# Attention and two feed-forward layers on one core: high parts of weights on GpSimd, and other costs in the planner

## The chip, the core and the metric

The kernel runs on one core of a Trainium2 chip. A core has five engines, each with a queue of its own that it works off in order: TensorE (PE, matrix products), VectorE (DVE), ScalarE (ACT), GpSimd (POOL) and SyncE (SP, which here only issues transfers). Transfers run on 16 DMA engines; they are issued by SyncE, ScalarE or GpSimd. Those that add to what lies at their destination ("accumulating" below) are issued by GpSimd. Matrix products are summed up in PSUM, in 8 banks of 512 columns.

The metric is the time of the device for one execution, in microseconds (us). Three runs of the kernel before took 522.79, 523.54 and 525.84 us; the median is 523.54.

## The reference

Attention over 2 batches, 12 heads, 448 positions and head size 64, with scores that are capped by a tanh, and then two feed-forward layers on 896 rows (2 x 448) of width 768 with 2048 hidden units, all in fp32:

```python
scores = cap * np.tanh((q @ k.T) / sqrt(64) / cap)
attn   = softmax(scores)                  # over keys
x      = (attn @ v)                       # 896 x 768
h = x @ w_in;   g = h * np.cos(h);              x = g @ w_out
h = x @ w_in2;  g = h * (1 / (1 + np.exp(-h))); y = g @ w_out2
```

## The kernel before, in words

The weights come as 64-bit numbers and are turned into fp32 on the chip. A fp32 product is made of three faster products: each operand is split into a high part, which TensorE's faster format holds, and a low part, which is what is left; high times high, high times low and low times high are added in the bank. A split is two instructions: a copy into the faster format (the high part, by ScalarE) and a subtraction (the low part, by VectorE). `split` (line 671) records both, with `n` columns for each of 128 partitions: 768 for a block of weights, 384 for half a one, 448 or 896 for activations.

The four feed-forward products are done in stages: `gemm_in` (first layer in), `gemm_out` (first layer out), `gemm_sums` (second in) and `gemm_last` (second out). Each uses a scheme of seven products in place of eight for blocks of 2 x 2 (Strassen's, in Winograd's form), so that sums of blocks of weights and of activations are made beforehand. These sums run on VectorE or, where a list says "DMA", as accumulating transfers that GpSimd issues (`plus`, line 477; the lists `WE`, `S1E`, `S3E`, `LE`, lines 604 to 611). One of the products of `gemm_out` is taken in plain fp32 without splits (`plain_product`).

From the end of attention on, nothing is issued directly. The stages record tasks (`do`, line 444): an engine, a cost, the values read and written, a due time. TensorE's tasks come one after the other at 202.8 ns for each 448 columns, and the due times of all others are worked out back from these. `run_plan` (line 512) then plays the tasks through: whenever an engine is free, it takes the task with the earliest due time whose inputs are there and for whose outputs buffers are free. The costs in it are formulas: `act` and `dve` (lines 471 and 474) for the two engines, `dma` (line 466) for transfers, and the table `LAT` for the time until others see a result. The order that comes out is the order in which instructions are issued on the chip; there they wait for semaphores, not for the planned times. So what the planner believes of a cost sets only the order.

In `gemm_in`, three pairs of weight blocks (p = 0, 1, 2) are multiplied plainly, with three products each; the others (p = 3 to 7) in the scheme of seven. For such a pair, `blocks` (line 862) makes four sums of half blocks, one after the other (`ADDS`), and splits in between: "A" before any sum, "S31" after two of them, "S24" after all four, "A22" besides. `m1` to `m7` (from line 976) are the seven products of a pair; `m1` ends with a ScalarE copy from one bank into another, in which `m2` goes on adding. In the trace, `v` are buffers of activations or of weights, `hl` those of a high or low part, `bank` a bank, `wx` two buffers for converted weights, `wraw` weights as loaded.

Of the kernel before, what the change touches and what calls it, by code (L numbers as in the profile page):

```python
# [38 lines left out]
def tile_attention_ffn_ffn(  # L39
# [401 lines left out]
    LAT = {"X": 0, "EW": 300, "PE": 280, "ACT": 210, "SP": 3500, "POOL": 300, "DVE": 170}  # L441
# [70 lines left out]
    def run_plan(free_at):  # L512
# [29 lines left out]
        while events:  # L542
# [15 lines left out]
            for e in LAT:  # L558
                if busy[e] > now or e == "EW":
                    continue  # L560
                for t in sorted(ready[e] + (ready["EW"] if e in ("POOL", "DVE") else []), key=lambda t: (t.dl, t.n)):
# [12 lines left out]
                    if t.eng == "EW":  # L574
                        t.eng, t.cost, t.lat = e, t.costs[e], LAT[e]
# [31 lines left out]
    DUE = [220000, 236000, 252000, 268000, 284000, 300000, 316000, 332000, 348000, 364000, 380000, 396000, 1000000000, 1000000000, 1000000000, 1000000000]  # L607
# [3 lines left out]
    S1E = [["DVE", "DMA"][n] for n in (1, 1, 0, 1, 0, 1, 0, 0)]  # L611
    HALF1 = [('half', 'ring'), ('half', 'half'), ('half', 'half'), ('ring', 'ring'), ('half', 'ring'), ('half', 'ring'), ('half', 'ring'), ('ring', 'ring')]
# [11 lines left out]
    PLAIN2 = (1, 0)  # L624

    def copy(out, src, scale=1.0):
        nc.scalar.activation(out=out, in_=src, func=AF.Copy, scale=scale)  # L627
# [103 lines left out]
    def plain_product(acc, key, w, d, gname):  # L731
        NQ, QW = HK + 1, 2
        fresh = key not in acc
        if fresh:
            acc[key] = [Val("bank") for _ in range(HK)]
        banks = acc[key]
        for q in range(NQ):
            t, subs = d[gname, q]
            for k in range(HK):
                def go(q=q, k=k, v=w[q], t=t):  # L740
                    for c in range(QW):
                        cols = slice(c * DH + k * P, c * DH + (k + 1) * P)
                        nc.tensor.matmul(banks[k].buf[:, :S], half_w(v)[:, cols], t.buf[:, c, :], start=fresh and q == 0 and c == 0, stop=q == NQ - 1 and c == QW - 1, skip_group_check=True)  # L743
                pe(3.69 * QW, go, [w[q], *subs], [banks[k]])

    def product(acc, key, w, d, gname, neg=False):
        NQ, QW = HK + 1, 2
        fresh = key not in acc
        if fresh:
            acc[key] = [Val("bank") for _ in range(HK)]  # L750
        banks = acc[key]
        for q in range(NQ):
# [12 lines left out]
    def gemm_out():  # L765
# [22 lines left out]
        if PLAIN2[0]:  # L788
            plain_product(acc, "A", x11, gx, "B11")
        else:  # L790
            product(acc, "A", x11, gx, "B11")
        if PLAIN2[1]:
            for d in range(HK):
                act(S, lambda d=d: copy(kc[d].buf[:, 0, :], bk("A", d)), [acc["A"][d]], [c11[d]])
            x12 = fresh("12")
            plain_product(acc, "B", x12, gx, "B21")
        else:
            acc["B"] = [Val("bank") for d in range(HK)]
            for d in range(HK):
                act(S, lambda d=d: copy(bk("B", d), bk("A", d)), [acc["A"][d]], [acc["B"][d]])  # L800
            x12 = fresh("12")
            product(acc, "B", x12, gx, "B21", True)
        sum_g(GE[0], gx, "B11", "B11", "B12")
        for d in range(HK):
            if PLAIN2[1]:
                dve(S, lambda d=d: sub_(kc[d].buf[:, 0, :], kc[d].buf[:, 0, :], bk("B", d)), [acc["B"][d]], [c11[d]], due=clock["pe"] + 1500)
            else:
                act(S, lambda d=d: copy(kc[d].buf[:, 0, :], bk("B", d)), [acc["B"][d]], [c11[d]], due=clock["pe"] + 1500)
            T["B11", d] = split_t((lambda d=d: kc[d].buf[:, 0, :]), [c11[d]])
# [10 lines left out]
        product(acc, "C", y, gx, "B11")  # L820
# [11 lines left out]
        product(acc, "A", x11, gx, "B12")  # L832
# [5 lines left out]
        product(acc, "C", x12, gx, "B22")  # L838
# [14 lines left out]
        product(acc, "A", x22, gx, "B21")  # L853
# [434 lines left out]
```

## Time and profile before

| | us |
|---|---|
| median of 3 runs | 523.54 (522.79 to 525.84) |
| the profiled execution | 523.46 |
| its span (first to last instruction) | 521.3 |
| TensorE busy | 512.3 |
| VectorE busy | 425.8 |
| ScalarE busy | 411.5 |
| GpSimd busy | 59.2 |

The profiled execution is the one that all rows below come from. Its time is that of the device; the span leaves out what lies before the first and behind the last instruction. The ends of matmuls are modelled, so a matmul's time is longer than the distance from its start to that of the next one, and TensorE's busy time says little; gaps are to be read from starts. A wait for several things is put down to the one that came last. The clock is what TensorE was granted, as a share of 2.4 GHz. A line such as L627 is often that of a helper which many parts of the kernel call (L627 the ScalarE copy, L630 VectorE's two-operand instruction, L686 the matmul of a split product, L743 that of the plain one).

### The profile page before, as it was taken

The numbers are of one execution on the slowest core, as the hardware profiler recorded it, in microseconds if no ns is written. First come the engines' busy times: TensorE is split into PE (matmuls) and PEld (weight loads), VectorE is DVE, ScalarE is ACT, GpSimd is POOL, SyncE is SP. The second block draws the span as 40 slices with busy tenths as digits, with TensorE's granted clock in tenths as the row PEclk, the third lists the DMA queues.
The fourth block names the chain that finished last, engine by engine and source line by source line (L and its number), as shares of the span: only waits on it lengthen the run. The fifth ranks groups of instructions, "written<-read, shape, count | busy, mean of one in ns | idle before, by whom it ended". The sixth has DMA issues, their size and how long they took to land.

```text
span 521.3 us, 7217 instructions
## 1 busy us (share of the span) xinstructions
PE 512.3 (98%) x2631; PEld 420.6 (81%) x2631; DVE 425.8 (82%) x599; ACT 411.5 (79%) x581; POOL 59.2 (11%) x82
## 2 busy tenths in 40 slices
PE   8999999999899999999999999999999999999997
PEld 5444443899799998589999999999999999999996
DVE  5388997899799789999999999977879888975660
ACT  6999997699799989999877577899999755556341
POOL 0145442001101000002100011000000013200000
PEclk9999999999989999999999999999999999999999
DMA  8146464296617117599913051969989974950111
GB/s 307 57 138 189 112 208 132 86 346 170 195 19 211 58 60 266 182 341 315 220 70 122 0 152 31 354 223 329 331 312 316 348 167 75 251 132 0 54 53 53
DMA packets 26983, 91.05 MB, mean 175 GB/s; under 512 B 4473, under 2 KB 9637, under 8 KB 26949
## 3 DMA queue, kind: packets, MB, share of 16 engines
q1 hardware_dynamic: 19488, 70.89, 38.4%
q0 software_dynamic: 7104, 19.40, 16.7%
q8 instruction: 20, 0.33, 0.2%
q10 hardware_dynamic: 356, 0.32, 0.2%
q14 instruction: 15, 0.11, 0.1%
HBM read 72.75 MB, written 10.66 MB: 160 GB/s over the span
## 4 chain that ended last, share of the span: by engine, by line
PE 86%; issue 7%; ACT 3%; DMA 2%; POOL 1%; DVE 0%; POOLq 0%; ACTq 0%
PE bank L686 68%; PE po L273 4%; PE sc L239 4%; PE bank L743 3%; DMA v<-v 2%; PE sc L243 2%; PE sm L291 2%; PE po L283 2%; ACT e L251 1%; PE warm L347 1%; ACT e L257 1%; POOL v L479 0%; ACT v L627 0%; POOL sums L312 0%; ACT hl L627 0%
## 5 line engine op out<-in xcount | busy, mean ns | idle before, releaser
L686 PE MATMUL bank<-v,hl 128*128 128x448 f32 x1440 | 299.2, 367 | 0.0
L686 PEld LDWEIGHTS bank<-v,hl 128*128 128x128 f32 x1440 | 270.8, 188 | 24.6 <-issue 0.7
L630 DVE TENSOR_TENSOR v<-v,v 128x896 fp32r<-128x896 f32 (+4 forms) x110 | 107.0, 996 | 27.6 <-ACT v L627 26.9
L627 ACT ACTIVATE v<-v 128x896 fp32r<-128x896 f32 (+2 forms) x81 | 67.9, 851 | 56.4 <-PE bank L686 54.9
L630 DVE TENSOR_TENSOR hl<-v,hl 128x768 fp32r<-128x768 f32 (+1 forms) x89 | 79.5, 899 | 12.6 <-ACT hl L627 11.2
L627 ACT ACTIVATE hl<-v 128x768 fp32r<-128x768 f32 (+1 forms) x89 | 70.2, 797 | 3.9 <-DMA v<-v 2.9
L686 PE MATMUL bank<-x,hl 128*128 128x448 f32 x297 | 63.1, 371 | 1.9 <-ACT bank L627 1.9
L686 PEld LDWEIGHTS bank<-x,hl 128*128 128x128 f32 x297 | 56.5, 191 | 7.6 <-ACT bank L627 2.3
L659 ACT ACTIVATE wraw<-wraw 128x768 int32<-128x768 uint8 x61 | 55.6, 919 | 3.4 <-DMA wraw<-in_moe_w_in 2.5
L627 ACT ACTIVATE v<-bank 128x448 f32<-128x448 f32 (+2 forms) x82 | 43.5, 539 | 17.0 <-PE bank L686 16.6
L662 ACT ACTIVATE wraw<-wraw 128x768 f32<-128x768 f32 x61 | 55.6, 916 | 0.0
L479 POOL DMA_DIRECT2D v<-v x24 | 22.5, 937 | 213.2 <-DVE hl L630 108.5
L251 ACT ACTIVATE e<-sc,scap 128x896 f32<-128x896 f32 (+1 forms) x48 | 40.1, 912 | 6.7 <-PE sc L239 6.7
L665 DVE SCALAR_TENSOR_TENSOR v<-wraw 128x768 int32<-128x768 int32 x40 | 37.8, 954 | 1.1 <-ACT wraw L662 0.6
L686 PE MATMUL bank<-v,v 128*128 128x448 f32 x180 | 38.4, 365 | 0.0
L686 PEld LDWEIGHTS bank<-v,v 128*128 128x128 f32 x180 | 33.8, 188 | 2.7
L257 ACT ACTIVATE e<-e,capt 128x3136 f32<-128x3136 f32 (+2 forms) x13 | 35.2, 2710 | 0.4
L273 PE MATMUL po<-e,vf 128*64 128x448 f32 x144 | 29.4, 540 | 0.4 <-ACT e L257 0.4
L273 PEld LDWEIGHTS po<-e,vf 128*64 128x64 f32 x144 | 10.2, 137 | 17.3 <-issue 16.3
L665 DVE SCALAR_TENSOR_TENSOR wx<-wraw 128x768 int32<-128x768 int32 x21 | 20.0, 954 | 4.4 <-ACT wraw L662 3.8
L630 DVE TENSOR_TENSOR v<-v 128x384 f32<-128x384 f32 (+1 forms) x42 | 23.4, 562 | 0.3
L312 POOL DMA_DIRECT2D sums<-xs x22 | 17.5, 800 | 50.4 <-DVE sums L318 41.8
(79 smaller groups left out, 470.1 us busy)
## 6 DMA issues: line engine op xcount, KB each, us to landing
wraw<-in_moe_w_out SPq DMA_DIRECT2D x32, 768.0 KB, 5.5
wraw<-in_moe_w_in SPq DMA_DIRECT2D x29, 768.0 KB, 5.9
wd<-wx SPq DMA_DIRECT2D x16, 384.0 KB, 5.4
v<-wd SPq DMA_DIRECT2D x16, 384.0 KB, 8.4
v<-v POOLq DMA_DIRECT2D x12, 384.0 KB, 8.4
raw<-in_qkv POOLq DMA_DIRECT2D x9, 480.0 KB, 4.4
v<-wd POOLq DMA_DIRECT2D x8, 384.0 KB, 6.5
rb<-rs SPq DMA_DIRECT2D x24, 112.0 KB, 3.2
```

Of the source, the lines that this page charges most:

```text
L239: nc.tensor.matmul(ps[:, u, :S], kk[rows, cols], qq[rows, :S], start=m == 0, stop=m == 2)
L251: nc.scalar.activation(out=e32[p][:, 2 * t:2 * t + n, :], in_=sc.pop((p, t))[:, :n, :S], func=AF.Tanh, scale=scap)
L257: nc.scalar.activation(out=e, in_=e, func=AF.Exp, scale=capt)
L273: nc.tensor.matmul(po[u * D:(u + 1) * D], vf[p][:, 2 * t + u, :], e32[p][:, 2 * t + u, :], start=first and n == 0, stop=last and n == len( ...
L312: (nc.gpsimd if p < NPT - 1 else nc.scalar).dma_start(sums[p][:, y], x[y * Q:y * Q + D + 1:D])
L479: dma("POOL", kb, lambda: nc.gpsimd.dma_start(o(), b(), accum_op=ALU.add), r, w, adds=True)
L627: nc.scalar.activation(out=out, in_=src, func=AF.Copy, scale=scale)
L630: nc.vector.tensor_tensor(out=out, in0=a, in1=b, op=op)
L659: nc.scalar.activation(out=b[:, :, 0], in_=b.bitcast(U8)[:, :, 3], func=AF.Copy, scale=1.0 / 32, bias=-0.5 + 1.0 / 64)
L662: nc.scalar.activation(out=w(1).bitcast(F32), in_=w(1).bitcast(F32), func=AF.Prelu, scale=2.0 ** -112, alpha=2.0 ** 32)
L665: nc.vector.scalar_tensor_tensor(out=view(), in0=w(1), scalar=3, in1=w(0), op0=ALU.logical_shift_left, op1=ALU.bitwise_or)
L686: nc.tensor.matmul(bank, x, y, start=first and m == 0, stop=last and m == len(ops) - 1, skip_group_check=True)
```

## The change

- In `split`, the copy that makes the high part, where it has 768 or 384 columns (weights), becomes a task of a kind of its own, "COPY". ScalarE may take it as before; GpSimd may take it where the task's due time lies far enough behind: later than now, plus the difference between the cost planned for GpSimd (2.7 us for 768 columns, 1.5 for 384) and that for ScalarE, plus 1.5 us. On GpSimd it is a multiplication by 1 or -1.
- In the planner, an accumulating transfer moves 160 instead of 200 GB/s and has a lag of 1700 instead of 600 ns; VectorE's formula has the factor 1.05 instead of 1.03.
- More sums are made by accumulating transfers: the last list of `WE` (4 transfers of 384 KB), the first pair of the second layer (`S3E`) and pair 4 of the first (`S1E`; 4 of 192 KB each).
- The due times of the conversions for the last stage (`DUE`) come at steps of 12 instead of 16 us. One pair takes its last split's buffers from another pool (`HALF1`).
- `plain_product` is merged into `product`, with a list of blocks that are multiplied whole; for the list that is set, the matmuls are the same.

```diff
-    LAT = {"X": 0, "EW": 300, "PE": 280, "ACT": 210, "SP": 3500, "POOL": 300, "DVE": 170}
+    LAT = {"X": 0, "COPY": 300, "PE": 280, "SP": 3500, "POOL": 400, "ACT": 210, "DVE": 170}
+    COSTS = {768: 2700, 384: 1500}
+    SPARE = 1500
...
-        rate = 0.2 if adds else 0.38 if kb > 450 else 0.24
+        rate = 0.16 if adds else 0.38 if kb > 450 else 0.24
         cost = 350 if eng == "SP" else 900 if adds else 600
-        do(eng, cost, fn, r, w, moves=kb * 1.024 / rate, lag=1700 if eng == "POOL" and not adds else 600, **k)
+        do(eng, cost, fn, r, w, moves=kb * 1.024 / rate, lag=1700 if eng == "POOL" else 600, **k)
...
-        do("DVE", 1.03 * (95 + (0.521 if one else 1.0417) * n), fn, r, w, **k)
+        do("DVE", 1.05 * (95 + (0.521 if one else 1.0417) * n), fn, r, w, **k)
...
-                for t in sorted(ready[e] + (ready["EW"] if e in ("POOL", "DVE") else []), key=lambda t: (t.dl, t.n)):
+                free = ready["COPY"] if e == "ACT" else [t for t in ready["COPY"] if t.dl > now + t.slow - t.cost + SPARE] if e == "POOL" else []
+                for t in sorted(ready[e] + free, key=lambda t: (t.dl, t.n)):
...
-                    if t.eng == "EW":
-                        t.eng, t.cost, t.lat = e, t.costs[e], LAT[e]
+                    if t.eng == "COPY":
+                        t.eng, t.cost, t.lat = e, t.slow if e == "POOL" else t.cost, LAT[e]
...
-    GE, WE, LE = [["DVE", "DMA"][n] for n in (0, 0, 0, 0)], [["DVE", "DMA"][n] for n in (0, 1, 1, 0)], [["DVE", "DMA"][n] for n in (0, 1)]
+    GE, WE, LE = [["DVE", "DMA"][n] for n in (0, 0, 0, 0)], [["DVE", "DMA"][n] for n in (0, 1, 1, 1)], [["DVE", "DMA"][n] for n in (0, 1)]
...
-    S3E = [["DVE", "DMA"][n] for n in (0, 1, 0, 0, 0, 0, 0, 0)]
+    S3E = [["DVE", "DMA"][n] for n in (1, 1, 0, 0, 0, 0, 0, 0)]
...
-    S1E = [["DVE", "DMA"][n] for n in (1, 1, 0, 1, 0, 1, 0, 0)]
+    S1E = [["DVE", "DMA"][n] for n in (1, 1, 0, 1, 1, 1, 0, 0)]
...
     def split(n, hi, lo, vhi, vlo, src, r, neg=False):
-        act(n, lambda: copy(vhi(), src(), -1.0 if neg else 1.0), r, [hi])
+        if n in COSTS:
+            def go():
+                if t.eng == "POOL":
+                    nc.gpsimd.tensor_scalar(out=vhi(), in0=src(), scalar1=-1.0 if neg else 1.0, scalar2=None, op0=ALU.mult)
+                else:
+                    copy(vhi(), src(), -1.0 if neg else 1.0)
+            t = do("COPY", 1.03 * (14 + 0.963 * n), go, r, [hi])
+            t.slow = COSTS[n]
+        else:
+            act(n, lambda: copy(vhi(), src(), -1.0 if neg else 1.0), r, [hi])
         dve(n, lambda: (neg_sub if neg else sub_)(vlo(), src(), vhi().bitcast(F32)), [hi, *r], [lo])
```

Since the planner sets the order, the change moves instructions on every engine. In all, 67 copies stand on GpSimd (58 of 768 columns, 9 of 384), and 12 sums more are accumulating transfers.

**ScalarE, pair 3 of the first layer.** Before: `hl_89<-v_1200` is the copy for the high part of "S24", which reads what four accumulating transfers made; `bank_1047<-bank_1045` is the copy at the end of `m1`.

```order
L659 ACTIVATE wraw_1385<-wraw_1385 128x768
L627 ACTIVATE hl_89<-v_1200 128x768
L963 ACTIVATE v_1454<-v_1454 128x448
L627 ACTIVATE v_1476<-bank_1044 128x448
L964 ACTIVATE v_1454<-v_1454 128x448
L627 ACTIVATE v_1480<-xv_68 128x448
L627 ACTIVATE v_1483<-xv_69 128x448
L627 ACTIVATE bank_1047<-bank_1045 128x448
```

After, from that same bank copy on, `hl_92<-v_1205` is the copy for "S24":

```order
L630 ACTIVATE bank_1047<-bank_1045 128x448
L955 ACTIVATE v_1482<-v_1482 128x448
L630 ACTIVATE v_1504<-xv_70 128x448
L956 ACTIVATE v_1482<-v_1482 128x448
L630 ACTIVATE v_1517<-bank_1046 128x448
L630 ACTIVATE v_1520<-xv_71 128x448
L630 ACTIVATE v_1523<-xv_72 128x448
L662 ACTIVATE wraw_1367<-wraw_1367 128x768
L630 ACTIVATE v_1391<-bank_1047 128x448
L630 ACTIVATE hl_92<-v_1205 128x768
```

The copy for "S24" stood six rows ahead of the bank copy and stands nine rows behind it.

**TensorE, the same place.** Each product is six rows of the order with nine matmuls; the first of each is shown. Before: `m2` of pair 3 (bank6), then `m6` of pair 3 (bank4), the first to read "S24" (hl2_89):

```order
L686 MATMUL bank6_1047<-x3_0_80,hl0_87 128x448 x2
...
L686 MATMUL bank4_1045<-v37_1350,hl2_89 128x448 x2
...
L686 MATMUL bank5_1046<-x3_1_81,hl2_89 128x448 x2
...
L686 MATMUL bank7_1048<-x0_0_74,v50_1420 128x448 x2
...
L686 MATMUL bank0_1041<-v10_1152,hl4_91 128x448 x2
```

After, from `m2` of pair 3 on; `m6` of pair 3 reads "S24" in hl5_92:

```order
L698 MATMUL bank6_1047<-x3_0_80,hl7_94 128x448 x2
...
L698 MATMUL bank7_1048<-x0_0_74,v29_1284 128x448 x2
...
L698 MATMUL bank0_1041<-v10_1151,hl1_88 128x448 x2
...
L698 MATMUL bank4_1045<-v51_1432,hl5_92 128x448 x2
...
L698 MATMUL bank5_1046<-x3_1_81,hl5_92 128x448 x2
```

Two products of pair 4 (bank7 and bank0) have moved ahead of `m6` of pair 3.

**GpSimd, the first feed-forward stage.** Before, from the end of attention on, only issues of accumulating transfers stand there (`v_1200` is pair 3, `v_1348` pair 5, the rest belong to `gemm_out`):

```order
L479 DMA v_1200<-v_1200 128x384 x4
L479 DMA v_1348<-v_1348 128x384 x4
L479 DMA v_2086<-v_1908 128x768
L479 DMA v_2106<-v_1931 128x768
L479 DMA v_1908<-v_2140 128x768
```

After, from the same point on (`v_1205` is pair 3, `v_1259` pair 4, `v_1353` pair 5, `wx` the plain pairs; the ISA row stands there once, ahead of the first copy):

```order
L678 ISA
L678 TENSOR_SCALAR hl_93<-wx 128x768
L678 TENSOR_SCALAR hl_88<-wx 128x768
L481 DMA v_1205<-v_1205 128x384
L678 TENSOR_SCALAR v_1284<-v_1259 128x768
L481 DMA v_1259<-v_1259 128x384
L481 DMA v_1205<-v_1205 128x384
L678 TENSOR_SCALAR hl_91<-wx 128x768
L481 DMA v_1259<-v_1259 128x384
L481 DMA v_1353<-v_1353 128x384
L481 DMA v_1205<-v_1205 128x384
```

Copies and the transfers of three pairs now stand in one queue, where those of two pairs stood alone.

## Rows read from the trace of the kernel before

**Rows 1.** The page's first part: busy us, share of the span, instructions.

```profile
PE 512.3 (98%) x2631; PEld 420.6 (81%) x2631; DVE 425.8 (82%) x599; ACT 411.5 (79%) x581; POOL 59.2 (11%) x82
```

**Rows 2.** The page's slices, 40 of equal length, busy tenths and granted clock.

```profile
PE   8999999999899999999999999999999999999997
...
PEclk9999999999989999999999999999999999999999
```

**Rows 3.** TensorE's timeline: start and length in us, then [idle time before <-releaser].

```profile
93.65 45.87 PE L686 MATMUL bank<-x,hl 128*128 128x448 f32 x225
139.35 1.99 PE L686 MATMUL bank<-v,hl 128*128 128x448 f32 x9
143.24 3.35 PE L686 MATMUL bank<-x,hl 128*128 128x448 f32 x9 [1.90 <-ACT bank L627]
146.39 2.33 PE L686 MATMUL bank<-v,hl 128*128 128x448 f32 x9
148.56 1.99 PE L686 MATMUL bank<-x,hl 128*128 128x448 f32 x9
```

**Rows 4.** Windows: busy time of each engine in a stretch.

```profile
core 0: us, PE busy (x) PEld busy (x) DVE busy (x) ACT busy (x) POOL busy (x), PEclk, DMA share, GB/s
...
143.00:150.00 7.00, 6.76 (x26) 6.10 (x27) 6.35 (x13) 6.61 (x14) 0.86 (x1) 0.76 0.17 29
197.00:223.00 26.00, 26.00 (x91) 17.00 (x90) 24.81 (x34) 25.97 (x43) 0.00 (x0) 1.00 0.67 233
223.00:311.00 88.00, 88.00 (x434) 81.23 (x433) 84.12 (x102) 68.22 (x94) 8.71 (x10) 1.00 0.58 172
```

**Rows 5.** ScalarE's timeline around the gap.

```profile
139.62 0.85 ACT L627 ACTIVATE hl<-v 128x768 fp32r<-128x768 f32 x1 [2.88 <-DMA v<-v]
...
142.66 0.53 ACT L627 ACTIVATE bank<-bank 128x448 f32<-128x448 f32 x1
```

**Rows 6.** The chain of waits before the gap: start us, us, what.

```profile
126.78 5.75 DMA v<-v
...
132.81 6.72 DMA v<-v
```

**Rows 7.** TensorE's timeline from the second stage on.

```profile
223.20 88.06 PE L686 MATMUL bank<-v,hl 128*128 128x448 f32 x432
311.10 1.99 PE L686 MATMUL bank<-v,v 128*128 128x448 f32 x9
...
384.00 133.75 PE L686 MATMUL bank<-v,hl 128*128 128x448 f32 x648
```

**Rows 8.** GpSimd's timeline: the first two accumulations of pair 3.

```profile
113.97 0.98 POOL L479 DMA_DIRECT2D v<-v  x1 [23.57 <-DVE hl L630]
119.24 0.88 POOL L479 DMA_DIRECT2D v<-v  x1 [4.28 <-DMA v<-v]
```

**Rows 9.** Groups by line and shape: busy us, mean ns, idle us before.

```profile
L630 DVE TENSOR_TENSOR hl<-v,hl 128x768 fp32r<-128x768 f32 x77 | 73.3, 953 | 12.4 <-ACT hl L627 11.2 <-issue 0.7 <-PE bank L686 0.4
L627 ACT ACTIVATE hl<-v 128x768 fp32r<-128x768 f32 x77 | 64.4, 839 | 3.9 <-DMA v<-v 2.9 <-DMA v<-wd 1.0
...
L479 POOL DMA_DIRECT2D v<-v x24 | 22.5, 937 | 213.2 <-DVE hl L630 108.5 <-DVE v L630 56.5 <-DMA v<-v 28.1
...
L627 ACT ACTIVATE hl<-v 128x384 fp32r<-128x384 f32 x12 | 6.3, 529 | 0.0
L222 DVE CAST qh<-raw 128x832 fp32r<-128x832 f32 x11 | 6.3, 573 | 0.0
...
L630 DVE TENSOR_TENSOR wx<-wx 128x384 f32<-128x384 f32 x4 | 2.2, 552 | 0.0
```

More of the change, by code (lines that the diff above doesn't have):

```diff
@@ L558, in run_plan @@
             for e in LAT:
-                if busy[e] > now or e == "EW":
+                if busy[e] > now or e == "COPY":
                     continue
-                for t in sorted(ready[e] + (ready["EW"] if e in ("POOL", "DVE") else []), key=lambda t: (t.dl, t.n)):
+                free = ready["COPY"] if e == "ACT" else [t for t in ready["COPY"] if t.dl > now + t.slow - t.cost + SPARE] if e == "POOL" else []
+                for t in sorted(ready[e] + free, key=lambda t: (t.dl, t.n)):
                     want = [v for v in t.vals if not v.held]
@@ L603, in tile_attention_ffn_ffn @@
     NORMS = 6900, 9700
[L604 removed]
+    GE, WE, LE = [["DVE", "DMA"][n] for n in (0, 0, 0, 0)], [["DVE", "DMA"][n] for n in (0, 1, 1, 1)], [["DVE", "DMA"][n] for n in (0, 1)]
     FE = "DVE"
[L606 to L607 removed]
+    S3E = [["DVE", "DMA"][n] for n in (1, 1, 0, 0, 0, 0, 0, 0)]
+    DUE = [220000, 232000, 244000, 256000, 268000, 280000, 292000, 304000, 316000, 328000, 340000, 352000, 1000000000, 1000000000, 1000000000, 1000000000]
     base_s = KF + 4 * (HK + 1)
     base_l = base_s + KF
[L611 to L612 removed]
+    S1E = [["DVE", "DMA"][n] for n in (1, 1, 0, 1, 1, 1, 0, 0)]
+    HALF1 = [('half', 'ring'), ('half', 'half'), ('half', 'half'), ('ring', 'ring'), ('half', 'ring'), ('half', 'ring'), ('half', 'half'), ('ring', 'ring')]
     low, high = range(KD - 2), range(KD - 2, KD)
@@ L621, in tile_attention_ffn_ffn @@
     ORDER1.append((4, HP - 1))
-    PLAIN2 = (1, 0)
+    WHOLE = ((0, 1, 2, 3), (), (), (), ())
     def copy(out, src, scale=1.0):
@@ L729, in sum_g, with product @@
                 dve(B * S, lambda t=t, x=x, y=y: sub_(fl(t), fl(x), fl(y), op), [*xs, *ys], ts)
-    def plain_product(acc, key, w, d, gname):
+    def product(acc, key, w, d, gname, neg=False, whole=()):
         NQ, QW = HK + 1, 2
@@ L737, in plain_product, with go @@
         for q in range(NQ):
[L738 to L752, printed above, removed]
+            if q in whole:
+                t, subs = d[gname, q]
+                for k in range(HK):
+                    def go(q=q, k=k, v=w[q], t=t):
+                        mms(banks[k].buf[:, :S], [(half_w(v)[:, c * DH + k * P:c * DH + (k + 1) * P], t.buf[:, c, :]) for c in range(QW)], fresh and q == 0, q == NQ - 1)
+                    pe(3.69 * QW, go, [w[q], *subs], [banks[k]])
+                continue
             whi_, wlo_, flat = split_w(w[q])
@@ L787, in gemm_out @@
         x11 = fresh("11")
[L788 to L802, printed above, removed]
+        product(acc, "A", x11, gx, "B11", whole=WHOLE[0])
+        acc["B"] = [Val("bank") for d in range(HK)]
+        for d in range(HK):
+            act(S, lambda d=d: copy(bk("B", d), bk("A", d)), [acc["A"][d]], [acc["B"][d]])
+        x12 = fresh("12")
+        product(acc, "B", x12, gx, "B21", True)
         sum_g(GE[0], gx, "B11", "B11", "B12")
         for d in range(HK):
[L805 to L808, printed above, removed]
+            act(S, lambda d=d: copy(kc[d].buf[:, 0, :], bk("B", d)), [acc["B"][d]], [c11[d]], due=clock["pe"] + 1500)
             T["B11", d] = split_t((lambda d=d: kc[d].buf[:, 0, :]), [c11[d]])
@@ L819, in gemm_out @@
             w_sum(WE[0], y[q], y[q], x21[q])
-        product(acc, "C", y, gx, "B11")
+        product(acc, "C", y, gx, "B11", whole=WHOLE[1])
         for d in range(HK):
@@ L831, in gemm_out @@
         sum_g(GE[2], gx, "B12", "B22", "B12")
-        product(acc, "A", x11, gx, "B12")
+        product(acc, "A", x11, gx, "B12", whole=WHOLE[2])
         for d in range(HK):
@@ L837, in gemm_out @@
             w_sum(WE[3], x12[q], x12[q], y[q])
-        product(acc, "C", x12, gx, "B22")
+        product(acc, "C", x12, gx, "B22", whole=WHOLE[3])
         for d in range(HK):
@@ L852, in gemm_out @@
         sum_g(GE[3], gx, "B21", "B11", "B21")
-        product(acc, "A", x22, gx, "B21")
+        product(acc, "A", x22, gx, "B21", whole=WHOLE[4])
         do("ACT", 1300, lambda: nc.scalar.activation(out=capt, in_=capt, func=AF.Silu), [], [table], due=clock["pe"] - 12000)
```

## The prediction

> **What bounds the kernel now.** I read the page's first part, the slices, TensorE's timeline, the windows, and then the timelines of the two engines that the first gap leads to. TensorE is busy 98% of the span, VectorE 82%, ScalarE 79%, GpSimd 11% [rows 1]. The slices show TensorE at nine tenths nearly everywhere and the granted clock in tenths at 9, but for one 8 in the twelfth slice (143 to 156 us) [rows 2]. So only gaps of TensorE can be won, and since a modelled matmul is longer than its pitch, I take them from starts in the timeline.
>
> In the feed-forward part the first 225 matmuls of 448 columns take 45.70 us from start to start (93.65 to 139.35), 203.1 ns each, so nine of them 1.83. Around the twelfth slice they don't: the nine that start at 139.35 are followed by nine at 143.24, which is 3.89 us; these take 3.15 us (to 146.39), the next nine 2.17 (to 148.56) [rows 3]. Against 1.83 the surplus is 2.06 + 1.32 + 0.34 = 3.72 us. The first part is the wait, named as a wait for a ScalarE copy of a bank. The rest is the clock: the window from 143 to 150 us was granted 0.76, the others shown 1.00 [rows 4]. That is a stretch at the lower of the two levels, 1.2 in place of 2.4 GHz, after TensorE had stood idle for 1.90 us.
>
> What ended last at that gap: ScalarE takes its work in order. The copy of the bank that TensorE wants is done at 142.66. Six rows of the program before it stands a copy that makes high parts (hl<-v, 768 columns); it could start only at 139.62, after 2.88 us of idle time, because an accumulating transfer had not landed [rows 5]. The chain of waits goes on from there: two accumulating transfers one after the other, 5.75 and 6.72 us from issue to landing, the second landing at 139.53 [rows 6]. So the gap is a transfer that lands later than the plan thought, with a short copy queued behind its reader.
>
> Elsewhere TensorE waits for nothing in this part. One thing remains: 432 matmuls from 223.20 take 87.90 us to the next group (203.5 ns each), but the last 648, from 384.00, take 133.75 (206.4) [rows 7]. No row gives a cause, so the sum leaves this as it is, and the range carries it.
>
> **The change, part by part.** *The order at the gap.* In the order of ScalarE before, the reader of the transfer (hl_89<-v_1200) stands six rows ahead of the bank copy (bank_1047<-bank_1045); now its successor (hl_92<-v_1205) stands nine rows behind that copy. TensorE's order has two more products, one of bank7 and one of bank0, between the product that the copy feeds and the first that reads those high parts, so they are wanted 2 x 1.83 = 3.7 us later. The wait of 2.06 us and the half clock behind it (1.66) go: -3.7 us.
>
> *What is late next.* The same four accumulations of this pair (192 KB each) stay transfers, and GpSimd issues them behind new work. The first goes out at 113.97, the second at 119.24, the third at 126.78 and the fourth at 132.81 [rows 6, 8]. Now the first stands behind two copies by GpSimd; the second of these waits until TensorE has freed a buffer, after 90 matmuls of the part, 93.6 + 90 x 0.203 = 111.9 us; with a copy of 0.84 to 2.7 us (below) the first transfer goes out at 112.7 to 114.6, about as before. The third waits for the split behind the second landing; ScalarE makes that split now after a copy of the bank that TensorE fills at 93.6 + 162 x 0.203 = 126.5, so the third goes out near 130, three us later than before. With the landings of 5.75 and 6.72 it lands near 136 and the fourth near 143. ScalarE's copy (0.84) and VectorE's subtraction (0.95) [rows 9] then end near 144.6. The product that wants them has 261 matmuls of this part before it: 93.6 + 261 x 0.2035 = 146.7. Two microseconds are left: enough, but not much.
>
> *Copies moved to GpSimd.* The order has 67 on GpSimd, 58 of 768 columns and 9 of 384. On ScalarE one of 768 takes 839 ns and one of 384 takes 529 [rows 9]: 58 x 0.84 + 9 x 0.53 = 53.5 us leave ScalarE. It is full (25.97 of 26 us) between 197 and 223 us [rows 4], yet TensorE doesn't wait there, so this gives nothing by itself; I cost it at 0. The trace shows no copy by GpSimd. The nearest rows are VectorE's cast of 832 columns, 573 ns, and ScalarE's copy [rows 9]; the upper end is the cost that the change itself plans with, 2.7 us. Where the copy is placed with slack its length costs nothing. That is the value I take, since the planner gives GpSimd a copy only where its due time lies 1.5 us or more behind the planned end.
>
> *Adds moved from VectorE to transfers.* 4 of 768 columns (953 ns, as the subtraction of that size) and 8 of 384 (552 ns) [rows 9]: 4 x 0.95 + 8 x 0.55 = 8.2 us off VectorE, and 12 more issues of 937 ns on GpSimd [rows 9]. GpSimd is idle 89% of the span, so the issues cost 0 so long as nothing that TensorE needs stands behind one; the cover is the two microseconds above.
>
> *VectorE assumed 1.05 in place of 1.03, accumulations slower, due times of the last weights earlier, buffers.* They move plans, not work: 0. The plain product is written anew with the same instructions (1520 rows of TensorE in both orders): 0.
>
> **The sum.** The profiled execution took 523.46 us for a span of 521.3 (2.2 around it), 0.08 below the median of 523.54. 523.46 - 3.72 = 519.74, and with the 0.08 519.8.
>
> **Rivals.** *The gap moves.* If GpSimd's queue or a landing is more than 2 us later than worked out, the product at 146.7 waits, and the clock falls again. A wait as long as the present one costs the whole 3.7 back: 523.5; half a wait without the clock some 1 us: 520.8. For it: every landing there is late against its plan, 36 accumulations are now issued in place of 24, and 67 copies stand in the same queue. Against: the plan now reckons with 0.16 and a longer lag per landing. Time: 522.4, between the two.
>
> *GpSimd and VectorE hold each other up; this is the slower side.* Between 223 and 311 us VectorE is busy 84.12 of 88 us [rows 4], nearly all of it with two operands that both lie in SBUF. Idle there: 3.9 us; four adds of 768 and four of 384 leave it, 6.0 us; together 9.9. By the tiles in the order, 19 copies by GpSimd fall to the products of that stretch. If a copy keeps VectorE from working for longer than 9.9 / 19 = 0.52 us, VectorE becomes the bound there. With ScalarE's 0.84 as the hold: 19 x 0.84 - 9.9 = 6.1 us, 526; with half of 2.7: 19 x 1.35 - 9.9 = 15.8, 535.6; with all of it 41 us, 561. Below nothing it can't be, since the copies do nothing for VectorE. For it: how full VectorE is. Against: no row shows a hold of either sign, since GpSimd computes nothing beside VectorE in this trace. Time: 531, the middle of the first two.
> The Trainium skill speaks for this rival: "SBUF — State Buffer", section "SBUF: two separate sides", says that a VectorE instruction with two SBUF inputs and a GpSimd instruction that reads SBUF take one port pair in turn, whole instruction by whole instruction, the other blocked. No row here can show it. By that rule each of the 19 copies holds VectorE for its own length and the time is that of the rival, 526 or more.
>
> *More is won.* If the slower pitch of the last 648 matmuls also goes, 648 x (206.4 - 203.5) ns = 1.9 us less: 517.9. If it sets in at 223 already, 432 x 2.9 ns = 1.3 us more: 521.1. For it nothing but that the pitch changed within one run.
>
> **How the numbers follow.** Forecast (gap gone, 519.8; own range 518.3 to 521.3): 0.54. Gap moves (522.4): 0.22. VectorE held up (531): 0.18. More is won (517.9): 0.06. Faster by over 0.5% (about what a measurement of this kernel can tell from no change) is below 520.9: 0.06, and 0.49 of the forecast's 0.54, and 0.03 of the second: 0.58. Slower is above 526.2: the third, but for 0.02 of its lower end: 0.16. Within: the rest, 0.26. The range goes from 517.4 to 528.5 and leaves out the upper part of the third case (0.12) and some 0.04 below.
>
> **What would show it.** Right: TensorE's timeline has no gap near 141 us, the clock is 1.00 in the window from 143 to 150, the bank copy comes before the transfer's reader on ScalarE, VectorE's subtraction of 768 keeps its 953 ns [rows 9]. The second case: a wait of TensorE on VectorE or ScalarE somewhere after 143 us, and a granted clock below 1.00 behind it. The third: VectorE's subtractions of 768 and 896 columns clearly longer while GpSimd copies, VectorE without idle time in 223 to 311, TensorE waiting for it. Wrong in another way: a wait for GpSimd itself, its copies far beyond 2.7 us.

## The result

The changed kernel took 528.01 us (median of 9 runs, 525.63 to 723.2) against 523.54 for the kernel before in the same series (9 runs): 1.0085 of its time, 95% interval 1.0063 to 1.0108. The forecast was 519.8. The one profiled execution of that series ran at a granted clock of 0.66 from end to end (723.2 us) and is left out of the ratio (the median of the other eight is 527.5). All rows "after" come from a repeat of the same kernel, which took 527.38 us (527.04 to 529.13), 1.0100 [1.0066, 1.0133].

The page of that repeat: busy time by engine, and TensorE's slices and clock.

```profile
span 525.4 us, 7351 instructions
PE 512.3 (98%) x2631; PEld 417.8 (80%) x2631; DVE 447.0 (85%) x587; ACT 369.1 (70%) x514; POOL 227.8 (43%) x161
...
PE   8999999999999999999889999999999999999997
...
PEclk9999999999999999999999999999999999999999
```

Against [rows 1, 2]: GpSimd has gone from 59 to 228 us and ScalarE from 412 to 369. VectorE has gone up, from 426 to 447, though it has 12 instructions less. The 8 in the clock's twelfth slice is gone; TensorE has two 8s in the middle instead, from 250 to 276 us.

TensorE's timeline after, at the old gap and from the second stage on (start, length, then idle time and what ended it):

```profile
138.89 1.99 PE L698 MATMUL bank<-v,hl 128*128 128x448 f32 x9
140.72 1.99 PE L698 MATMUL bank<-x,hl 128*128 128x448 f32 x9
142.54 1.98 PE L698 MATMUL bank<-x,v 128*128 128x448 f32 x9
...
219.49 33.75 PE L698 MATMUL bank<-v,hl 128*128 128x448 f32 x164
253.40 3.91 PE L698 MATMUL bank<-v,hl 128*128 128x448 f32 x18 [0.16 <-DVE hl L633]
259.01 3.91 PE L698 MATMUL bank<-v,hl 128*128 128x448 f32 x18 [1.70 <-DVE hl L633]
264.76 14.66 PE L698 MATMUL bank<-v,hl 128*128 128x448 f32 x71 [1.83 <-DVE hl L633]
280.08 32.98 PE L698 MATMUL bank<-v,hl 128*128 128x448 f32 x161 [0.66 <-DVE v L633]
```

The gap of [rows 3] has closed: nine products take 1.83 and 1.82 us where they took 3.89. The stretch from 223 to 311 us, in which TensorE waited for nothing before [rows 7], now has four waits, all for VectorE. Three smaller ones follow at 331 to 333 and 474 us (one of 0.43 us for GpSimd, the others for VectorE); all seven cost 7.5 us from start to start.

VectorE and GpSimd after, grouped by line and shape (busy us, mean ns of one, then idle time before), which answers to [rows 9]:

```profile
L678 POOL TENSOR_SCALAR hl<-v 128x768 fp32r<-128x768 f32 x52 | 136.8, 2674 | 97.7 <-PE bank L698 58.6 <-DVE v L668 29.0 <-DVE v L633 5.7
L633 DVE TENSOR_TENSOR hl<-v,hl 128x768 fp32r<-128x768 f32 x76 | 78.2, 1034 | 8.8 <-ACT hl L630 3.5 <-POOL hl L678 2.9 <-PE bank L698 2.4
L668 DVE SCALAR_TENSOR_TENSOR v<-wraw 128x768 int32<-128x768 int32 x40 | 43.4, 1089 | 1.9 <-ACT wraw L665 1.8
L633 DVE TENSOR_TENSOR v<-v,v 128x896 f32<-128x896 f32 x32 | 41.6, 1318 | 0.1
```

The subtraction of 768 columns went from 953 to 1034 ns on the mean. For GpSimd's results it waited only 2.9 us in this group, and 2.0 in one more, so the copies are hardly late; VectorE itself is slower. Where it loses time is seen in its own timeline, here with the rows of GpSimd's for the same stretch below it:

```profile
250.76 1.71 DVE L636 SCALAR_TENSOR_TENSOR v<-v,v 128x896 fp32r<-128x896 f32 x1
252.40 0.95 DVE L633 TENSOR_TENSOR hl<-v,hl 128x768 fp32r<-128x768 f32 x1
...
259.75 1.08 DVE L636 SCALAR_TENSOR_TENSOR v<-v,v 128x896 fp32r<-128x896 f32 x1
```

```profile
247.07 3.75 POOL L678 TENSOR_SCALAR hl<-v 128x768 fp32r<-128x768 f32 x1
249.15 3.44 POOL L481 DMA_DIRECT2D v<-v  x2
250.31 5.01 POOL L678 TENSOR_SCALAR hl<-v 128x768 fp32r<-128x768 f32 x1
252.79 4.30 POOL L481 DMA_DIRECT2D v<-v  x2
253.96 5.50 POOL L678 TENSOR_SCALAR hl<-v 128x768 fp32r<-128x768 f32 x1
```

The same form takes 1.71 us at 250.76, while a copy runs, and 1.08 at 259.75, when the last has ended (259.46). The copies take 3.75 to 5.5 us in this stretch, where one takes 2.13 undisturbed; that is not VectorE's doing alone, since the spans of the issues of transfers (L481) overlap theirs. A place without such issues shows the two engines by themselves, VectorE first, then GpSimd; the last row is the longest copy of all:

```profile
477.50 1.08 DVE L633 TENSOR_TENSOR v<-v,v 128x896 fp32r<-128x896 f32 x1
478.50 1.58 DVE L633 TENSOR_TENSOR hl<-v,hl 128x768 fp32r<-128x768 f32 x1
480.00 1.08 DVE L633 TENSOR_TENSOR v<-v,v 128x896 fp32r<-128x896 f32 x1
```

```profile
477.86 2.72 POOL L678 TENSOR_SCALAR hl<-v 128x768 fp32r<-128x768 f32 x1 [1.66 <-PE bank L698]
...
267.60 6.25 POOL L678 TENSOR_SCALAR hl<-v 128x768 fp32r<-128x768 f32 x1
```

The copy begins 0.72 us before VectorE's add ends and takes 0.59 us more than 2.13. VectorE's next instruction takes 1.58 in place of 0.95. The one after it begins at 480.00, inside the copy's span, and takes its usual 1.08. This holds through the whole run: 35 copies of 768 columns overlap no issue of a transfer, and each of them takes 2.13 us plus what VectorE's work on SBUF still needed when the copy began, less 0.13, to within 0.011 us. (The copy at 267.60 fits too: five instructions of VectorE ran on until 271.85.) So a copy waits for VectorE's running instruction to its end, and then holds VectorE's next one up, by 0.62 us where that would follow at once. That is much less than the copy's own span.

### The profile page after: what moved, and what is told of

Read it like the earlier page. It is cut to its first block, busy times and chain, and to the rows that moved or that the text cites. A ratio compares the mean times of both kernels' runs of the same rounds, so it can differ in the third digit from the quotient of the medians.

```text
span 721.4 us, 7351 instructions
## 1 busy us (share of the span) xinstructions
PE 715.6 (99%) x2631; PEld 461.7 (64%) x2631; DVE 432.0 (60%) x587; ACT 375.9 (52%) x514; POOL 211.9 (29%) x161
## 4 chain that ended last, share of the span: by engine, by line
PE 99%; DVE 0%; issue 0%; ACT 0%; ACTq 0%
PE bank L698 82%; PE po L273 6%; PE sc L239 5%; PE sc L243 2%; PE sm L291 2%; PE po L283 2%; PE warm L347 1%; DVE e L299 0%; DVE zero L356 0%; DVE v L1218 0%; ACT v L630 0%; PE sm L284 0%; DVE sums L318 0%; DVE xs L310 0%; DVE sums L319 0%
## 5 line engine op out<-in xcount | busy, mean ns | idle before, releaser
L698 PE MATMUL bank<-v,hl 128*128 128x448 f32 x1431 | 413.5, 466 | 0.0
L698 PEld LDWEIGHTS bank<-v,hl 128*128 128x128 f32 x1431 | 296.6, 207 | 112.5 <-issue 0.7
L678 POOL TENSOR_SCALAR hl<-v 128x768 fp32r<-128x768 f32 (+1 forms) x60 | 127.7, 2129 | 269.2 <-PE bank L698 187.9
L698 PE MATMUL bank<-v,v 128*128 128x448 f32 x237 | 83.8, 524 | 0.0
L698 PE MATMUL bank<-x,hl 128*128 128x448 f32 x288 | 83.8, 467 | 0.0
L698 PEld LDWEIGHTS bank<-v,v 128*128 128x128 f32 x237 | 49.5, 209 | 31.5 <-issue 16.4
L481 POOL DMA_DIRECT2D v<-v x32 | 28.7, 966 | 59.3 <-DVE hl L633 45.0
L273 PE MATMUL po<-e,vf 128*64 128x448 f32 x144 | 43.9, 756 | 0.0
L633 DVE TENSOR_TENSOR v<-bank,v 128x448 f32<-128x448 f32 x28 | 17.2, 622 | 27.2 <-PE bank L698 27.2
L305 DVE COPY xu<-po 128x448 f32<-128x448 f32 x12 | 7.5, 624 | 42.6 <-PE po L283 40.7
```

The costliest lines, as they stand in the source:

```text
L273: nc.tensor.matmul(po[u * D:(u + 1) * D], vf[p][:, 2 * t + u, :], e32[p][:, 2 * t + u, :], start=first and n == 0, stop=last and n == len( ...
L481: dma("POOL", kb, lambda: nc.gpsimd.dma_start(o(), b(), accum_op=ALU.add), r, w, adds=True)
L633: nc.vector.tensor_tensor(out=out, in0=a, in1=b, op=op)
L678: nc.gpsimd.tensor_scalar(out=vhi(), in0=src(), scalar1=-1.0 if neg else 1.0, scalar2=None, op0=ALU.mult)
L698: nc.tensor.matmul(bank, x, y, start=first and m == 0, stop=last and m == len(ops) - 1, skip_group_check=True)
```

## The experiments

**Theory:** a copy on GpSimd reads SBUF, that holds VectorE, and where VectorE is full TensorE waits. **Rivals:** GpSimd's copies or transfers come too late; the order that the planner makes for three engines is worse by itself; the new costs are what loses. Ratios are to the kernel before on the same chip in the same series, with 95% intervals.

**The change repeated (r1_after).**

> The changed kernel again, for a profile at the full clock. The nine runs so far lie at 525.6 to 529.4 us, and some of them had a granted clock of 1.000, so no wait of TensorE of 2 us can be in all of them. Theory A (GpSimd's copies hold VectorE up): the subtractions of 768 and the adds of 896 columns are longer than 953 and 1087 ns while GpSimd copies, VectorE has no idle time between 223 and 311 us, and TensorE waits for it by 4 to 8 us in sum. Theory B (TensorE's pitch): no waits, but the stretch with 206.7 ns for each matmul of 448 columns sets in long before 398 us; from 143 us on that is up to 1700 x 4 ns = 7 us. Theory C (the gap has moved): one or two waits of TensorE on ScalarE or VectorE behind an accumulating transfer, 2 to 4 us each.

527.38 us, 1.0100 [1.0066, 1.0133]; its rows are above. Theory A came, in the durations and in the waits (7.5 us). Not all of it: from 223 to 311 us VectorE is busy 83.98 of 88, without idle time only up to 265 (its windows stand with the break-even below).

**No copy on GpSimd (r2_nopool):** everything else of the change is kept.

```diff
-  free = ready["COPY"] if e == "ACT" else [t for t in ready["COPY"] if t.dl > now + t.slow - t.cost + SPARE] if e == "POOL" else []
+  free = ready["COPY"] if e == "ACT" else []
```

> The changed kernel with all high parts made by ScalarE again; the rest of the change stays (slower transfers and VectorE in the planner, 12 more sums by transfers, due times, buffers). Theory A: the copies were the loss; about 520 us (the gap at 141 us closed). Theory C: the loss is in the transfers and the order; 525 to 529 us as with the whole change. Theory B says nothing certain: the time follows the pitch, 520 where it is as before.

519.78 us (519.37 to 520.41), 0.9947 [0.9927, 0.9967]: what had been forecast for the change, and faster than both kernels. VectorE's additions of 896 columns take 1084 ns on the mean in place of 1318, and in the windows the clock is 1.00 where it was 0.76 in [rows 4] (columns as there):

```profile
143.00:150.00 7.00, 7.00 (x37) 6.50 (x36) 5.70 (x10) 7.00 (x14) 0.44 (x1) 1.00 0.18 29
223.00:311.00 88.00, 88.00 (x435) 81.17 (x434) 79.68 (x96) 68.95 (x97) 15.92 (x18) 1.00 0.67 180
```

**The copies alone (r3_poolonly):** the kernel before with the "COPY" tasks of the change; the old rate and lag, the old lists.

```diff
-    LAT = {"X": 0, "EW": 300, "PE": 280, "ACT": 210, "SP": 3500, "POOL": 300, "DVE": 170}
+    LAT = {"X": 0, "COPY": 300, "PE": 280, "SP": 3500, "POOL": 300, "ACT": 210, "DVE": 170}
+    COSTS = {768: 2700, 384: 1500}
+    SPARE = 1500
...
```

> The kernel before with only the copies that GpSimd may take; the planner's other costs, the lists of sums made by transfers, due times and buffers are those of before. Theory A: 526 to 530 us. Theory C: the copies alone do no harm; 520 to 524 us. Theory B: slower only if the stretch with the longer pitch grows with GpSimd's copies.

537.67 us, 1.0312 [1.0254, 1.0370], well above theory A's 526 to 530. The copies (77 here) lose 3%, and the rest of the change wins back about two thirds of it. Here too VectorE's 896 columns take 1353 ns, and TensorE waits 2.57 us for it at 264.81. But it also waits for ScalarE, 1.62 us at 313.72 and 2.05 at 329.53, so this run doesn't price the hold of VectorE alone.

**The same order, the copies on ScalarE (r4_actplace):** all 67 stand where they stood, but ScalarE makes them. The orders on VectorE and TensorE are the same, row by row, as in the changed kernel.

```diff
-                    nc.gpsimd.tensor_scalar(out=vhi(), in0=src(), scalar1=-1.0 if neg else 1.0, scalar2=None, op0=ALU.mult)
+                    copy(vhi(), src(), -1.0 if neg else 1.0)
```

> The changed kernel with its planned order, word for word the same on TensorE and VectorE, but each of the 67 copies planned for GpSimd is issued on ScalarE at the same place of the plan. Hold theory (a copy by GpSimd makes VectorE's instructions beside it longer; in the repeat of the changed kernel by 27 us over 67 copies, 0.41 us each): VectorE's adds of 896 columns fall from 1318 to 1085 ns, the waits of TensorE on VectorE between 252 and 281 us go, 519.5 to 521 us. Order theory (the order that the planner made is bad in itself): 526 to 529 us, with the same waits.

523.63 us, 1.0022 [0.9995, 1.0049], between the two expectations: the durations are those of the hold theory (1086 ns for 896 columns), the time is not. Since VectorE does the same 587 instructions in the same order, each can be set against its twin. 535 agree within 50 ns; 48 are over 200 ns longer in the changed kernel, 31.3 us in all, and every one of the 48 overlaps a copy on GpSimd. The commonest surplus is 0.6 us (26 of them); the nine above 0.8 us stand beside copies whose spans overlap the issue of an accumulating transfer by 0.27 us or more. Of the instructions that run beside a copy, the 31 that have an operand in PSUM (a bank) are none of them longer; of the 151 others, 103 are not longer either, most of which ran already when the copy began or came after its hold. In all VectorE loses 29.7 us to 67 copies, 0.44 us each. The waits at 252 to 280 us are gone here but for 0.2 us at 279, but ScalarE has no room for the copies at the old place:

```profile
139.22 1.99 PE L698 MATMUL bank<-v,hl 128*128 128x448 f32 x9
143.30 3.59 PE L698 MATMUL bank<-x,hl 128*128 128x448 f32 x9 [2.09 <-ACT bank L630]
146.73 1.99 PE L698 MATMUL bank<-x,v 128*128 128x448 f32 x9
```

This is the gap of [rows 3] again, with its half clock (nine products in 3.43 us; granted 0.76 from 143 to 150 us). So at one and the same order the engine of the copies is worth 0.8%, and r4 and r2 together say that an order made for three engines is poor for two.

**Each copy twice (r5_twice):** the instruction on GpSimd is issued a second time.

```diff
+                    nc.gpsimd.tensor_scalar(out=vhi(), in0=src(), scalar1=-1.0 if neg else 1.0, scalar2=None, op0=ALU.mult)
```

> The changed kernel with each copy by GpSimd issued twice, the second onto the same place; the same order elsewhere. Hold theory: VectorE's busy time grows by about 27 us more and, since it has under 3 us to spare between 220 and 285 us, where 15 or more copies stand, TensorE waits there by 6 us or more in addition: 534 to 545 us. Late theory (VectorE isn't held, but the copies come late and VectorE waits for them): VectorE's durations stay as in the repeat, its idle time waiting for GpSimd grows; 530 to 540 us.

586.99 us, 1.1226 [1.1175, 1.1277], far beyond both expectations. Here lateness joins in: VectorE's subtractions wait 50.4 us for GpSimd, against 2.9, and are longer too, so this run shows no more than that GpSimd's time is anything but free.

```profile
L633 DVE TENSOR_TENSOR hl<-v,hl 128x768 fp32r<-128x768 f32 x76 | 91.8, 1212 | 53.4 <-POOL hl L679 50.4 <-ACT hl L630 3.0
```

**Writing without reading (r6_memset):** GpSimd sets the high part to zero, which reads nothing, and ScalarE then makes the copy.

```diff
-                    nc.gpsimd.tensor_scalar(out=vhi(), in0=src(), scalar1=-1.0 if neg else 1.0, scalar2=None, op0=ALU.mult)
+                    nc.gpsimd.memset(vhi().bitcast(F32), 0.0)
+                    copy(vhi(), src(), -1.0 if neg else 1.0)
```

> The changed kernel with its order, where GpSimd only sets the tile to zero (768 or 384 columns written, nothing read) and ScalarE then makes the copy. If VectorE is held by GpSimd's reads alone, its adds of 896 columns take 1085 ns and the time is 520 to 524 us, ScalarE waiting here and there for a setting that comes late. If GpSimd's writes hold it too, the adds stay above 1150 ns and the time is 524 us or more.

525.51 us, 1.0057 [1.0033, 1.0081], with a wait of 1.31 us for ScalarE at 142.77, where r4 has its own. The time is above the 520 to 524 of the first expectation, so the durations decide. The groups by line and shape:

```profile
L633 DVE TENSOR_TENSOR hl<-v,hl 128x768 fp32r<-128x768 f32 x76 | 71.9, 952 | 6.0 <-ACT hl L630 3.2 <-PE bank L699 2.4
L678 POOL MEMSET hl<- 128x768 f32 x55 | 48.4, 902 | 185.3 <-PE bank L699 169.3 <-ACT v L1059 6.5 <-ACT hl L630 6.4
...
L633 DVE TENSOR_TENSOR v<-v,v 128x896 f32<-128x896 f32 x32 | 34.1, 1085 | 0.1
```

VectorE takes 952 and 1085 ns, as without any GpSimd work (953 and 1084 in r2). The 67 writes fill 56 us of GpSimd's time, the 67 copies 166; at the copies' rate of loss VectorE would have lost 10 us (56 / 166 x 29.7), and it lost nothing. So writing alone does not hold it, and the reading is what the copies do besides. The Trainium skill says so in "SBUF — State Buffer", section "SBUF: two separate sides": a VectorE instruction with two SBUF inputs meets a GpSimd instruction at their common ports only if that one reads SBUF. The PSUM operands of r4 agree as well. The same section of the Trainium skill has the one that starts first keep the ports for its whole instruction. For VectorE's instructions the trace agrees, since the 35 copies above wait to their end; for the copies it doesn't, since one of 2.13 us holds VectorE for 0.62 (0.30 where it has 384 columns). The measurement decides.

**Fewer copies (r7_spare):** the room asked for goes from 1.5 to 5 us; 19 copies stay on GpSimd.

```diff
-    SPARE = 1500
+    SPARE = 5000
```

> The changed kernel with 5 us of slack asked for in place of 1.5: 19 copies by GpSimd in place of 67, none of them between 220 and 285 us among the products of the second stage but one. Hold theory: 19 x 0.41 = 8 us of VectorE's time, outside the full stretch; 519.5 to 522 us. Order theory: no forecast; late theory: 520 to 523 us.

522.0 us, 0.9992 [0.9967, 1.0016]: between r2 and the change, and slower than r2. It lies at the upper end of the hold theory's range and inside the late theory's, so it doesn't tell them apart.

**Copies only where VectorE has room (r8_outside):** none is given to GpSimd between 132 and 255 us of the planner's time; 45 stay.

```diff
+    LO, HI = 132000, 255000
...
-  free = ready["COPY"] if e == "ACT" else [t for t in ready["COPY"] if t.dl > now + t.slow - t.cost + SPARE] if e == "POOL" else []
+  free = ready["COPY"] if e == "ACT" else [t for t in ready["COPY"] if t.dl > now + t.slow - t.cost + SPARE] if e == "POOL" and not LO < now < HI else []
```

> The changed kernel, but the planner gives GpSimd no copy between 132 and 255 us of its own time (TensorE's second stage and the beginning of the third, some 225 to 345 us of the trace): 45 copies stay on GpSimd in place of 67. Theory (a copy's read of SBUF holds VectorE, and that costs only where VectorE is full): the waits of TensorE on VectorE at 252 to 263, 279 and 331 us go, the rest stays (the one wait near 474 us of 0.2 us, the gap at 141 us closed), so 519.5 to 521, VectorE's additions of 896 columns in 225 to 310 us back at 1085 to 1090 ns, and VectorE's subtractions still longer outside. Rival (each copy costs the same wherever it stands, or the order made for three engines is the loss): two thirds of the copies keep two thirds of the loss against the kernel without copies on GpSimd, 519.8 + 0.67 x 7.6 = 524.9.

521.84 us (521.21 to 523.33), 0.9989 [0.9971, 1.0007]. A little above the theory's range, and 3 us from the rival's 524.9: leaving out a third of the copies, those of the full stretch, took away nearly three quarters of the loss against r2 (1.1 of 1.5%). The order differs from that of the changed kernel, so the share is a rough one. VectorE's additions of 896 columns from 223 to 311 us take 1136 ns, not quite the 1085 to 1090 expected (1367 in the changed kernel), those of the whole run 1229. Of TensorE's waits one is left in the stretch:

```profile
261.83 8.38 PE L699 MATMUL bank<-v,hl 128*128 128x448 f32 x40 [0.79 <-DVE hl L634]
```

**The costs alone (r9_costs):** the kernel before with the new rate and lags and VectorE's 1.05.

```diff
-    LAT = {"X": 0, "EW": 300, "PE": 280, "ACT": 210, "SP": 3500, "POOL": 300, "DVE": 170}
+    LAT = {"X": 0, "EW": 300, "PE": 280, "ACT": 210, "SP": 3500, "POOL": 400, "DVE": 170}
...
-        rate = 0.2 if adds else 0.38 if kb > 450 else 0.24
+        rate = 0.16 if adds else 0.38 if kb > 450 else 0.24
...
-        do(eng, cost, fn, r, w, moves=kb * 1.024 / rate, lag=1700 if eng == "POOL" and not adds else 600, **k)
+        do(eng, cost, fn, r, w, moves=kb * 1.024 / rate, lag=1700 if eng == "POOL" else 600, **k)
...
-        do("DVE", 1.03 * (95 + (0.521 if one else 1.0417) * n), fn, r, w, **k)
+        do("DVE", 1.05 * (95 + (0.521 if one else 1.0417) * n), fn, r, w, **k)
```

> The kernel before with the planner's costs alone (accumulating transfers 160 GB/s and a lag of 1700 ns, GpSimd's lag 400, VectorE's factor 1.05); no copies on GpSimd, the old lists of sums, due times and buffers. Theory (the gap at 141 us closes because the planner now knows how late the accumulations land): no wait above 0.5 us near 141 us, clock 1.00 in 143 to 150, 519.5 to 520.5. Rival (it takes the new lists, above all those of pair 4 and of the second layer): a gap of 1 to 2 us stays somewhere in 120 to 150 us, with a dip of the clock behind it, 522 to 524.

523.77 us, 1.0012 [0.9993, 1.0032]. Both expectations missed. The gap does close, by the costs alone, and the time stays:

```profile
138.88 1.99 PE L686 MATMUL bank<-v,hl 128*128 128x448 f32 x9
140.71 2.03 PE L686 MATMUL bank<-x,hl 128*128 128x448 f32 x9
142.57 2.01 PE L686 MATMUL bank<-x,v 128*128 128x448 f32 x9
...
219.12 89.79 PE L686 MATMUL bank<-v,hl 128*128 128x448 f32 x432
```

The 432 products that took 87.90 us in [rows 7] take 89.63 here (from 219.12 to the next group's start at 308.75): 207.5 ns each in place of 203.5. In all these traces the products of 448 columns mostly lie either 202 to 203 or 206 to 207 ns apart, and change over within a run. What they take beyond 202.7 ns, summed over all starts that are 150 to 250 ns apart, is 2.6 us in the kernel before, 3.2 in the changed one, 2.8 in r2, 4.1 in r4 and 5.5 here. So r9 wins 3.7 at the gap, loses 2.9 to the slow pitch and 1.7 to new waits at 314 and 328 to 331 us: +0.9, and the distance from the first to the last product has grown by 1.0 (423.7 to 424.7).

**One product more (r10_plain64, r11_fast64):** r2 with a product of 64 columns into a fresh bank of the last stage, overwritten by the next; once in plain fp32, once in the faster format (without the two `.bitcast(F32)`).

```diff
+                    if fresh and q == 0 and k == 0 and key == "C" and d is gf:
+                        nc.tensor.matmul(banks[0].buf[:, :64], ops[0][0].bitcast(F32), ops[0][1][:, :64].bitcast(F32), start=True, stop=True, skip_group_check=True)
```

> The kernel without copies on GpSimd, with one product more: 64 columns in plain fp32 into a fresh bank of the last stage (near 425 us), which the next product overwrites. In all traces so far TensorE's starts are 202.7 or 206.7 ns apart, and the slow pitch ended at the plain products near 220 us and at pauses (at 473.5 us in the changed kernel after 0.16 us). Theory (any break of the rhythm ends the slow pitch): the starts are 203 ns apart from 425 us to the end, about 430 products x 4 ns = 1.7 us less, plus 0.1 to 0.2 for the product itself: 518.2 to 518.6 where the kernel without it took 519.8. Rival (what is read or written sets the pitch): it stays at 206.5, 519.9.

> As r10_plain64, with the 64 columns in the faster format, as all products about it. If only the change of format ends the slow pitch: 206.5 ns to the end and 519.9; if any break of the rhythm does: 518.2 to 518.6.

518.22 us, 0.9922 [0.9895, 0.9948], and 518.74, 0.9933 [0.9909, 0.9957] (r10, r11). The end of TensorE's timeline, first without the product (r2), then with it (r11):

```profile
380.23 133.88 PE L698 MATMUL bank<-v,hl 128*128 128x448 f32 x648
```

```profile
380.03 59.48 PE L698 MATMUL bank<-v,hl 128*128 128x448 f32 x288
439.35 0.19 PE L767 MATMUL bank<-v,hl 128*128 128x64 f32 x1
439.38 73.19 PE L698 MATMUL bank<-v,hl 128*128 128x448 f32 x360
```

r2's 648 products take 206.6 ns each; behind the small one the 360 take 203.3. In r10 they take the same (73.20 us). Either format does it, so it isn't the change of format but the break in the row of equal products that ends the slow pitch here. Not every break does so for long: in r9 the wait at 314 us brought the fast pitch back for some 6 us only. Both beat the kernel before and the changed one; against r2 (0.9947) the ratios are lower by 0.25 and 0.14%, within the intervals, so there the timeline is the evidence: from first to last product r11 takes 419.0 us, r2 420.7. r10's profiled execution, its slowest of seven (520.68 us), takes 420.5; it lost elsewhere what it gained behind the small product.

## Why the prediction was wrong

**What bounds the kernel, and the order at the gap: right.** The wait of 2.06 us and the half clock are gone in the changed kernel and in r2, and r2 took 519.78 where 519.8 was forecast. The sum is not right to that digit: between first and last product r2 won 3.1 us rather than 3.7 (423.7 to 420.7), since short waits at 140 and 256 us came in (0.29 and 0.17) and the pitch cost 0.2 more. r9 shows which edit closes the gap: the planner's costs do, which the prediction had put at nothing by themselves.

**What is late next: right, by a narrow margin.** The copies and transfers of pair 3 in one queue did not make the product wait that was reckoned at 146.7; the first rival (the gap moves, 522.4) did not come. But the split ended at 146.15 us, not at 144.6, and the product began to read it at 146.19: of the two microseconds of cover less than half a microsecond was left for the low part.

**Adds moved off VectorE: right in kind.** VectorE's busy time from 223 to 311 us is 79.68 us in r2, against 84.12 in [rows 4]: 4.4 us less, where 6.0 had been reckoned.

**Copies moved to GpSimd: the step that failed.** "Where the copy is placed with slack its length costs nothing. That is the value I take." The length of a copy cost nothing indeed: only 4.9 us of VectorE's idle time and 0.4 of TensorE's went to waiting for GpSimd. What cost was the hold on VectorE while a copy reads, 29.7 us of VectorE's time, which the planner doesn't know of. Put at nothing, it cost 7.5 us against r2. The second rival had this mechanism with a chance of 0.18, and its 531 was 3 us too high. It alone brings the measured time into the upper end of the stated range; the forecast itself was of a faster kernel.

Its break-even held, with other sizes. It set 19 copies against 9.9 us of idle time from 223 to 311 us, 0.52 us a copy. In r4, whose order is the same, VectorE has 7.7 us free there (the sum of its windows below), and in the changed kernel its instructions of that stretch take 12.3 us more beside 18 copies: 0.68 us each, above the break-even, while the average over all 67 is 0.44. That is 4.6 us too much, near the 5.4 that TensorE's four waits cost. The rival's prices of 0.84 and more for each copy were too high. Nor does the idle time lie where the copies do. The windows of the changed kernel, then of r4, whose order is the same:

```profile
223.00:243.00 20.00, 20.00 (x101) 18.53 (x100) 20.00 (x20) 15.89 (x22) 14.47 (x9) 1.00 0.93 293
243.00:265.00 22.00, 18.31 (x88) 16.00 (x87) 22.00 (x18) 9.86 (x13) 16.41 (x12) 1.00 1.07 210
265.00:311.00 46.00, 45.34 (x223) 41.54 (x223) 41.98 (x49) 25.17 (x36) 30.03 (x16) 1.00 0.37 109
```

```profile
223.00:243.00 20.00, 20.00 (x98) 18.07 (x97) 19.92 (x22) 19.17 (x27) 1.74 (x2) 1.00 0.96 323
243.00:265.00 22.00, 22.00 (x110) 20.39 (x109) 20.86 (x23) 16.89 (x23) 8.87 (x10) 1.00 1.07 238
265.00:311.00 46.00, 46.00 (x227) 42.37 (x227) 39.48 (x52) 32.58 (x48) 5.28 (x6) 1.00 0.48 130
```

From 223 to 265 us VectorE (its busy time is the third behind the stretch's length) would have 1.2 us free of 42 (r4), and with 8 copies it has none. Against their twins in r4 its instructions there take 7.8 us more, 0.98 us a copy. The 6.5 us of room lie from 265 to 311 us, mostly too late.

**The balance.** From first to last product: 423.7 us before, 428.2 after. The gap gave 3.7; all seven waits took 7.5 and the pitch 0.6: +4.4, against 4.5 measured. The copies alone, against r2, cost 7.5 us: 7.0 in waits, 0.4 in pitch, the rest unassigned.

**Planner costs at nothing; more is won.** The first, as a sum, hid two things of either sign: the gap that closes, and a pitch that changes with every order. The slow pitch of [rows 7] turned out to be removable (r10, r11), but nothing in the change removes it.

Open: why the row of products falls into the slow pitch; why a copy of 2.13 us holds VectorE for 0.62 only; and why the hold is longer (up to 1.2 us) where an issue of a transfer overlaps the copy.

## What to carry to other kernels

An engine that is idle is not free if its work holds up a full one: before moving work, ask what the new engine reads while the other works, and count the hold (here 0.6 us a copy) as the other's time. Set the loss against idle time in the very stretch where the work lands (here 42 us with 1.2 free, not 88 with 7.7). To tell a hold from lateness, keep the order and change only the engine: twins of the same instruction then show it one by one.

## What the runs showed of the hardware

- GpSimd copies 768 columns of fp32 in 2.13 us where nothing disturbs it (384 in 1.17) and in up to 6.25 us beside VectorE, whose running instructions it waits out; a memset of 768 columns takes 0.90 us.
- A copy that reads SBUF holds up VectorE's next instruction whose operands lie in SBUF, by 0.62 us where it follows at once (0.30 for 384 columns), and by up to 1.2 where the issue of an accumulating transfer overlaps it. 48 instructions were held so (47 have two inputs, one is a cast); 31 beside a copy with an operand in PSUM were not lengthened at all.
- TensorE's products of 448 columns run at a pitch of 203 or 207 ns at a full granted clock (1.00). One product of 64 columns in between brought back the fast pitch for the 73 us to the end, as did a wait of 0.15 us in the changed kernel (233 products in 47 us from 474.26); across kernels it is worth up to 3 us in 520.
